# Two thirds of the r, k and v loads in rows of sixteen tokens, and a second set of decay tables

## The chip, the cores and the metric

The kernel runs on one core of a Trainium2 chip. The metric is the device time of one execution in microseconds (us), lower is better. Three executions of the kernel before took 121.07, 121.30 and 121.99 us (median 121.3).

The engines are named as in the profile: PE (TensorE, matmuls and transposes; PEld is its weight load), DVE (VectorE), ACT (ScalarE), POOL (GpSimd) and SP (which here only issues DMAs). All of them read and write the on-chip memory (SBUF); PE writes its results to a small second memory (PSUM), from which DVE and ACT copy them out ("eviction"). Sixteen DMA engines move data between HBM and SBUF.

## What is computed

The reference runs a linear-attention layer (r, k, v of 4 batches x 8 heads x 768 tokens x 48, a decay w and a bonus u per head and channel) and feeds its output, as 3072 tokens of 384 features, to a soft mixture of 8 experts with 4 slots each:

```python
for t in range(S):                                   # S = 768
    cur = einsum('bhd,bhe->bhde', u * k[t], v[t])
    y[t] = einsum('bhd,bhde->bhe', r[t], state + cur)
    state = w * state + einsum('bhd,bhe->bhde', k[t], v[t])
x = y as [3072, 384]
logits = x @ phi                                     # [3072, 32]
slot_input = softmax(logits over tokens).T @ x       # [32, 384]
slot_out[e] = relu(slot_input[e] @ w1[e]) @ w2[e]    # F = 1024, 8 experts
out = softmax(logits over slots) @ slot_out          # [3072, 384]
```

r, k and v are 14.2 MB together, w1 and w2 25.2 MB, the output 4.7 MB, all f32 in HBM.

## The kernel before

**Units.** The attention is computed in 12 units of 256 tokens, three to a batch, all heads together. A unit is two chunks of 128 tokens. For each unit n the tasks are, in the kernel's names (a task's letter, then the unit):

- `Lk Lr Lv`: three loads of 384 KB, issued by SP (line 188). A load has 32 rows of 8 tokens for each head, so it moves 256 pieces of 8 x 48 x 4 = 1536 B.
- `Sk Sr`: k and r times a table of decay powers, f32 to bf16 (line 376; on POOL, only `Sk0` on DVE). `VC`: v to bf16 (lines 402 and 404, on ACT or POOL).
- `Tk Tr Tv`: eight PE transposes each into a PSUM bank (lines 386, 412); `Ek Er Ev`: eviction to SBUF (line 328 on ACT, 326 on DVE); `PR`: the product of k and r for the bonus term (line 395, DVE).
- `N`/`NE` and `V`/`VE`: transposes back to token rows, and their eviction.
- `A`: the chunk's 128 x 128 scores, half a unit at a time (`An0`, `An1`, line 451), into one PSUM tile `Ab`; `K`: those times the causal mask, to bf16 (line 457, DVE, 24 in all).
- `U`, `SM`, `SI`, `SE`: the state's step (lines 471 to 496). `DV`: the bonus term (line 501, DVE). `Y`: the outputs (lines 513 to 524); `YE`: their eviction; `X`/`XE`: transposes for the mixture.

When a batch is through, its logits and both softmaxes follow (`L`, `ZC`, `RM`, `EX`, `NM`, `DP`, `AC` and others); `NM` ends in line 654 on DVE. After the last batch come the experts: `H` (first layer, line 803), `R`, `HT`, `HE`, and then `Q00` to `Q14` (second layer, line 848), of which `Q10` reads the second-layer weights of experts 4 and 5 (`W12`, `W13`), `Q11` those of expert 6 (`W14`), and `Q12` to `Q14` the three parts of the last one (`W15a`, `W15b`, `W15`). Then the output is computed and stored (lines 855 to 882).

**Order.** The string `ORDER` (lines 9 to 31) lists every task once; each engine runs its own tasks in that order, and `_Plan.run` (line 60) hands out the buffers in it. `Fn_m` are fillers: matmuls with no use (line 794), m/2 of 512 columns each. No engine overtakes within its own list, so a task that waits holds all that stands behind it on its engine.

**Loads and weights.** SP issues the loads in order and holds back when eight are under way. The weights (`W0` to `W15`, 768 KB each in bf16, converted by the DMA) are issued by POOL, between its other tasks. `W0` stands behind a one-element copy that waits until the v of unit 9 has landed (`GU = 9`, line 706, and line 713), so that the weights come behind the inputs; `W8` and later also wait for the weight DMA eight places earlier. Loads and weights share the buffers `raw`: 16, and the table's, which becomes free at the end.

**The start.** The table is built on chip: w arrives, ACT takes its logarithm, DVE multiplies it with exponents 0 to 8 plus the row's offset (line 256), ACT takes exponentials (lines 259 and 260). POOL waits for the last of these before `Sr0`, DVE for the first ones before `Sk0`. `CC`, `CT`, `CA`, `CU` and `CW` turn w and u into columns: `CC` (line 265) and `CA` (line 287) on DVE, `CT` on PE, `CU` (lines 290 and 291) on POOL, `CW` on ACT. `CB` (lines 313 and 314, with two ACT copies) makes constants for the mixture.

```python
        O(sp.dma_start(out=dst.rearrange("p (e x) -> p e x", e=2),
                       in_=a[b].rearrange("h (y j) d -> y h (j d)", j=J)[CC * R * i:CC * R * (i + 1)]))
...
            add(f"S{nm}{n}", "DVE" if n == i == 0 else "POOL", f_scale, deps=[f"L{nm}{n}"],
```

Of the kernel before, what the change touches and what calls it, by code (L numbers as in the profile page):

```python
# [9 lines left out]
Lk0 CB Lr0 Sk0 Tk0 Lv0 Sr0 Lk1 VC0:ACT Sk1 LU Lr1 Ek0 Sr1 F0_4 N0 Lv1 Tr0 Lk2 Lr2 Tv0 Er0 NE0:ACT CC Lv2 A01 CT  # L10
Ev0:ACT V0 VC1:ACT Lk3 PR0 CA K01 Lr3 VE0:ACT Tk1 A00 Tv1 CU Ek1 Sk2 Ev1:ACT Sr2 K00 Tr1 Lv3 Lk4 N1 CW LP Lr4 Sk3 U0
PR1 V1 Lv4 Er1 NE1:ACT VC2:ACT Tk2 A10 DV0 SM0 VE1:ACT Tv2 SI0 Lk5 Tr2 Y0 K10 Ek2 Sr3 SE0 A11 Ev2:ACT Lr5 K11 Sk4 U1
N2 Lv5 Er2:ACT PR2 Sr4 YE0 Lk6 Lr6 SM1 DV1 Lv6 VC3:ACT Lk7 Lr7 NE2:ACT VC4 Tk3 Sk5 A21 Ek3:ACT Lv7 Lk8 Tr3 Lr8
Er3:ACT Lv8 V2 Tv3 K21 SI1 Ev3:ACT Y1 Lk9 PR3 VC5 Lr9 Lv9 A31 SE1 Lk10 N3 V3 VE2:ACT YE1 Tk4 U2 K31 Lr10 CB0 VE3:ACT
Sk6 NE3 SM2 DV2 X10 Tr4 A20 Ek4:ACT XE10:ACT N4 U3 Tk5 Er4:ACT K20 A30 NE4:ACT PR4 K30 Tv4 Tv5 Ek5:ACT X00 Sr5 Y2
Lv10 Ev4:ACT VC7 A40 Tk6 Lk11 XE00:ACT CB1 N5 DV3 Ev5 SM3 Tr5 YE2 Y3 Ek6:ACT V4 NE5:ACT X20 K40 Lr11 SI3 PR5 Er5 YE3
A41 XE20 Tv7 VE4:ACT Sr6 VC6:ACT V5 SE3 Ev7:ACT VE5:ACT U4 K41 Tv6 SM4 DV4 Ev6:ACT L0 Lv11 Sk7 A50 W0 W1 RM0 N6 SI4
Tr6 ZC0 Tk7 K50 NE6:ACT EX0 A51 W2 SE4 ZT0 U5 Ek7:ACT V6 PR6 Sk8 Sr7 SU0 SM5 N7 Er6:ACT V7 K51 Y4 VE6:ACT A61
NE7:ACT VE7:ACT DV5 AL0 VC8 Sr8 VC9 Tk8 ET0 YE4 K61 Tr7 Sr10 U6 Ek8:ACT EE0:ACT A60 PR7 Er7:ACT Tv8 DP0 LC0 W3 SM6
SI6 K60 Y5 Ev8:ACT Sk9 AC0 A71 SE6 YE5 DV6 N8 NM0 Tv9 Tr8 NE8:ACT Ev9:ACT U7 LX0 Er8:ACT V8 LE0:ACT Y6 VE8:ACT YE6  # L20
Sr9 W4 K71 SM7 A80 PR8 W5 Sk11 X50 W6 XE50:ACT K80 SI7 Tk9 X30 Ek9 A70 XE30:ACT X40 N9 XE40:ACT NE9:ACT K70 Tr9 DV7
A81 SE7 L1 RM1 Sk10 VC10 Er9:ACT W7 W8 Tk11 Y7 Ek11:ACT ZC1 YE7 AL1 K81 U8 V9 PR9 VE9:ACT Tk10 N11 VC11 SM8 NE11:ACT
W9 A90 Sr11 Ek10:ACT Tr10 DV8 ZT1 K90 U9 Er10:ACT SU1 Tv10 A101 EX1 Ev10:ACT ET1 Y8 SM9 PR10 K101 W10 V10 N10 A91
W11 EE1:ACT VE10:ACT NE10:ACT W12 DV9 DP1 X60 W13 SI9 K91 Tr11 SE9 XE60:ACT A100 PR11 K100 U10 SM10 DV10 YE8 Tv11
Er11:ACT Y9 Ev11:ACT A110 K110 V11 YE9 X80 SI10 Y10 A111 VE11:ACT SE10 X70 AC1 U11 K111 SM11 XE80:ACT YE10 XE70:ACT
X90 DV11 L2 F1_3 X100 LC1 Y11 XE90:ACT XE100:ACT RM2 ZC2:DVE ZT2 AL2 L3 EX2 YE11 F2_2 X111 NM1 W14 ZC3 SU2 X110
XE111:ACT RM3 F3a_3 ET2 XE110 W15a LB4 EE2 W15b AL3 EX3 ET3 DP2 RM4 G1 EX4 G2 LC2 EE3 ET4 AC2 EE4:ACT G3 AL4 G5 DP3
AC3 DP4 GS AC4 LX1 ZT3 F4a_2 MG LE1:ACT UN F5_6 H11 H10 R11:DVE R10 H00 NM2 HT11 R00:DVE HE11 SU3 F6a_1 H01 R01:DVE
W15 LC3 LX2 HT10 F7a_1 HT00 LE2:ACT NM3 LT4 HT01 SU4 HE00 F8a_7 Q00 LX3 LC4 HE10 HE01:ACT Q01 F9_38 Q10 NM4 LX4
F10_11 Q11 F11_2 Q12 F12_2 Q13 Q14 LE4:ACT LE3  # L30
# [51 lines left out]
def kernel(  # L82
# [13 lines left out]
    B, H, S, D = r.shape  # L96
# [54 lines left out]
    pr_t = [cst.tile([128, PH, C], bf, name=f"pr{j}") for j in range(2)]  # L151
# [34 lines left out]
    def load_f(dst, a, n):  # L186
        b, i = divmod(n, U3)
        O(sp.dma_start(out=dst.rearrange("p (e x) -> p e x", e=2),
                       in_=a[b].rearrange("h (y j) d -> y h (j d)", j=J)[CC * R * i:CC * R * (i + 1)]))

# [52 lines left out]
    O(dve.tensor_copy(turn[:].rearrange("p (c q r) -> p c q r", c=CC, q=nQ), ident[:].rearrange("p (c r q) -> p c q r", c=CC, q=nQ)))  # L243
# [68 lines left out]
    def consts_b():  # L312
        O(dve.tensor_reduce(out=sel[:], in_=ident_f[:].rearrange("p (b c) -> p c b", b=B), axis=AX.X, op=ALU.add))
# [6 lines left out]
    L = _Plan(dict(raw=raw, ks=ks_t, kT=kT_t, rT=rT_t, vT=vT_t, vj=vj_t, kn=kn_t, vn=vn_t, AT=AT_t, pr=pr_t, dv=dv_t,  # L320
# [40 lines left out]
    add("CB", "DVE", lambda t: consts_b())  # L361
    xB, xTB = {}, {}
    for n in range(NU):
# [45 lines left out]
        def f_turn(t, vjb=vjb, Tb=Tb):  # L409
            src = vjb.inst[:].rearrange("p j e d -> p j (e d)")  # L410
            for jj in range(J):
                O(pe.transpose(Tb.inst[0:P2, jj * 128:(jj + 1) * 128], src[:, jj, :], turn[:]))  # L412
# [500 lines left out]
```

## Time and profile before

| | us |
|---|---|
| runs, median (lowest to highest) | 121.3 (121.07 to 121.99) |
| the profiled execution | 122.07 |
| its span in the trace | 120.3 |
| busy: PE, DVE, ACT, POOL | 102.4, 92.4, 81.8, 61.4 |
| granted PE clock, mean | 0.972 |
| DMA queue of the loads and stores (q1): 11208 packets, 18.93 MB | 43.9% of 16 engines |
| DMA queue of the weights (q0): 2592 packets, 12.58 MB written | 51.3% |

The profile is one execution of the program, recorded by the hardware. Its page lists the busy time of each engine; the span in 40 slices of 3.0 us with a digit for each engine's busy share; the DMA queues; the chain of work that ended last; and the costliest groups of instructions with what ended the idle time before them. The trace behind it can also be asked for the timeline of one engine (start, length, line, tiles, how many instructions, and idle time before it with what ended it) and for busy time, DMA share and GB/s in stretches of one's choice. The weights' GB/s count what is written as bf16; twice as much is read.

### The profile page before, as it was taken

To read this page: it belongs to the slowest core of one execution; us is meant where nothing else is said; L and a number is where in the kernel's file an instruction comes from. 1 tells how busy PE (TensorE), PEld (TensorE's weight loads), DVE (VectorE), ACT (ScalarE), POOL (GpSimd) and SP (SyncE) were. 2 spreads that over 40 slices of the span, in tenths; PEclk is the share of its full clock that TensorE was granted. 3 is DMA by queue.
4 is the path that set the end of the run, shared out by engine and by line. 5 is a ranking of instruction groups with operands and counts; after the bars stand their busy time and mean duration, and the time that the engine had idled before them with its cause. 6 is when DMAs were issued, how large, how long until landed. Compare 5 with 4: busy or idle time off the path is not lost.

```text
span 120.3 us, 4049 instructions
## 1 busy us (share of the span) xinstructions
PE 102.4 (85%) x1726; PEld 75.7 (63%) x1732; DVE 92.4 (77%) x175; ACT 81.8 (68%) x132; POOL 61.4 (51%) x75
## 2 busy tenths in 40 slices
PE   4987789999999899959999999999989999897000
PEld 1346668888888688758887788764436556673000
DVE  6947998999999999999999999988598100189000
ACT  4638699999989899869999799896235001188000
POOL 7368999999993999999996111011000000000000
PEclk9999999999999999999999999999999999999855
DMA  2999999999999999999999999999999997039994
GB/s 35 291 346 393 374 349 366 374 375 375 373 375 370 362 245 205 227 205 218 208 220 217 206 224 206 218 217 214 217 210 224 204 209 141 14 133 415 407 419 196
DMA packets 13961, 31.81 MB, mean 264 GB/s; under 512 B 1528, under 2 KB 11000, under 8 KB 13944
## 3 DMA queue, kind: packets, MB, share of 16 engines
q0 software_dynamic: 2592, 12.58, 51.3%
q1 hardware_dynamic: 11208, 18.93, 43.9%
q8 instruction: 13, 0.21, 0.7%
q10 hardware_dynamic: 144, 0.05, 0.2%
q14 instruction: 4, 0.03, 0.1%
HBM read 39.42 MB, written 4.72 MB: 367 GB/s over the span
## 4 chain that ended last, share of the span: by engine, by line
PE 61%; DVE 20%; ACT 7%; issue 3%; POOL 1%; DVEq 0%; POOLq 0%
PE T L386 7%; PE T L794 6%; PE Ab L451 5%; PE T L541 4%; PE T L412 4%; DVE AT_all L457 4%; PE T L426 3%; PE T L212 3%; PE Yb L518 3%; PE Yb L848 3%; PE Yb L513 2%; PE T L436 2%; PE Mb L848 2%; PE Yb L524 2%; DVE mix L880 2%
## 5 line engine op out<-in xcount | busy, mean ns | idle before, releaser
L376 POOL TENSOR_TENSOR mix<-raw,tabs 128x768 bf16<-128x768 f32 x23 | 41.7, 1831 | 3.6 <-DMA raw<-in_r_dram 2.4
L457 DVE TENSOR_TENSOR AT_all<-Ab,mask 128x1024 bf16<-128x1024 f32 x24 | 29.1, 1214 | 0.7 <-PE Ab L451 0.7
L328 ACT COPY mix<-T 128x1024 bf16<-128x1024 bf16 x17 | 17.0, 1030 | 0.2 <-PE T L386 0.2
L386 PE MATMUL T<-turn,mix 128*128 128x128 bf16 x192 | 15.0, 222 | 0.1
L386 PEld LDWEIGHTS <-mix 128*128 128x128 bf16 x192 | 12.0, 99 | 1.7 <-DVE mix L376 0.7
L717 POOL DMA_DIRECT2D raw<-in_moe_w_dram x10 | 5.4, 540 | 14.2 <-DMA raw<-in_moe_w_dram 14.2
L328 ACT COPY vT_all<-T 96x1024 bf16<-96x1024 bf16 x11 | 11.2, 1018 | 1.3 <-PE T L412 1.2
L501 DVE TENSOR_TENSOR dv<-vn,Mb 128x768 bf16<-128x768 bf16 x12 | 11.3, 942 | 0.0
L451 PE MATMUL Ab<-mix 64*128 64x128 bf16 x192 | 9.7, 218 | 1.8 <-DVE AT_all L457 0.7
L328 ACT CAST x<-Yb 128x768 bf16<-128x768 f32 x12 | 9.8, 814 | 0.7 <-PE Yb L524 0.6
L328 ACT COPY vn<-T 128x768 bf16<-128x768 bf16 x12 | 9.7, 810 | 0.6 <-PE T L436 0.6
L328 ACT COPY xT_all<-T 128x768 bf16<-128x768 bf16 (+1 forms) x11 | 8.6, 780 | 0.9 <-PE T L541 0.9
L856 DVE CAST so<-Mb 128x192 bf16<-128x192 f32 x1 | 0.4, 358 | 11.0 <-PE Mb L848 11.0
L328 ACT COPY LexpT<-T 128x768 bf16<-128x768 bf16 (+1 forms) x4 | 2.8, 693 | 8.7 <-PE T L697 8.7
L794 PE MATMUL T<-mix,ident 128*128 128x512 bf16 (+1 forms) x31 | 8.1, 373 | 0.3 <-issue 0.2
L451 PEld LDWEIGHTS <-mix 64*128 64x128 bf16 x192 | 5.8, 94 | 4.1 <-issue 2.2
L395 DVE TENSOR_TENSOR pr<-T,mix 128x1024 bf16<-128x1024 bf16 x12 | 8.2, 679 | 0.0
L328 ACT COPY kn<-T 128x768 bf16<-128x768 bf16 (+1 forms) x11 | 7.6, 694 | 0.4 <-PE T L426 0.3
L412 PE MATMUL T<-turn,vj 128*96 128x128 bf16 x96 | 7.4, 221 | 0.5 <-ACT vj L402 0.5
L518 PEld LDWEIGHTS <-AT_all 128*128 128x128 bf16 x192 | 6.6, 96 | 1.6
L426 PE MATMUL T<-ident,mix 128*128 128x128 bf16 x80 | 6.5, 219 | 0.4 <-DVE mix L326 0.4
L518 PE MATMUL Yb<-vn,AT_all 128*128 128x48 bf16 x192 | 6.8, 183 | 0.0
(173 smaller groups left out, 231.5 us busy)
## 6 DMA issues: line engine op xcount, KB each, us to landing
raw<-in_moe_w_dram POOLq DMA_DIRECT2D x15, 768.0 KB, 15.6
raw<-in_k_dram SPq DMA_DIRECT2D x12, 384.0 KB, 8.2
raw<-in_r_dram SPq DMA_DIRECT2D x12, 384.0 KB, 7.9
raw<-in_v_dram SPq DMA_DIRECT2D x12, 384.0 KB, 8.1
out_dram<-mix SPq DMA_DIRECT2D x3, 768.0 KB, 4.8
out_dram<-tabs SPq DMA_DIRECT2D x1, 768.0 KB, 6.7
out_dram<-AT_all SPq DMA_DIRECT2D x1, 768.0 KB
out_dram<-mix SPq DMA_DIRECT2D x1, 576.0 KB, 2.8
```

The source lines that it names most:

```text
L328: O(act.copy(dst, src))
L376: O(eng.tensor_mul(ks.inst.rearrange("p (j e s) -> p e j s", j=J, e=2)[:, :, :, 0:D], halfs(kb)[i].rearrange("p (e j d) -> p e j d", e=2, ...
L386: O(pe.transpose(Tb.inst[:, jj * 128:(jj + 1) * 128], src[:, jj, :], turn[:]))
L395: O(dve.tensor_mul(pb.inst[:].rearrange("p g (j r) -> p g j r", j=J), Tb.inst[:].rearrange("p (j g r) -> p g j r", j=J, r=R), kT.inst.rear ...
L412: O(pe.transpose(Tb.inst[0:P2, jj * 128:(jj + 1) * 128], src[:, jj, :], turn[:]))
L426: O(pe.transpose(Tb.inst[:, x * 128:(x + 1) * 128], kT.inst[:, x, :], ident[:]))
L451: O(pe.matmul(Abf.inst[:, e, x * C:(x + 1) * C], kT.inst[s, g * nQ + x, :], rT.inst[s, g * nQ + x, :]))
L457: O(dve.tensor_mul(AT.inst[:], Abf.inst[:].rearrange("p e (g t) -> p e g t", g=nQ), mask[:, None, None, :].to_broadcast([128, 2, nQ, C])))
L501: O(dve.tensor_mul(dvb.inst[:].rearrange("p g e d -> p (g e) d"), vn.inst[:].rearrange("p g e d -> p (g e) d"), Mf.inst[:, 448:448 + 2 * P ...
L518: O(pe.matmul(y[:, x // nQ, q * P2 + e * D:q * P2 + (e + 1) * D], a[x // nQ].inst[:, e, q, :], vn.inst[:, x, e, :], start=False, stop=(c = ...
L794: O(pe.matmul(o[:, 0:256 * min(n, 2)], ident[:], mix[:, 0:256 * min(n, 2)], start=True, stop=True))
L848: O(pe.matmul(SO[h][32 * x:32 * x + 32, :], hT[g][:, y, 32 * x:32 * x + 32], w2_of(g * EG + x)[:, y, h * Dm // 2:(h + 1) * Dm // 2], start ...
```

## The change

- Batches are loaded in two pieces in place of three: the first unit (256 tokens) as before in rows of 8 tokens (loads 0, 2, 4, 6), the second and third unit together in rows of 16 tokens (loads 1, 3, 5, 7): 768 KB each, 256 pieces of 3072 B. There are 24 loads in place of 36, with the same bytes.
- A long load is scaled, transposed and evicted in two halves `a` and `b`, eight of each row's sixteen tokens each. Both units of it need both halves.
- Rows of sixteen need exponents 0 to 16, and one table each for k and r (`tabl`), beside the short one (`tabs`). They are built by two more products on DVE (`AHa`, `AHb`, two instructions each) and four exponentials on ACT (`TB0a`, `TB1a`, `TB1b`, `TB0b`), inside the order.
- The buffers of transposed k, r and v are one for the short and one double one for the long load: three units' worth, where k and r had four and v two. `raw` has 14 buffers; the three tables' space is used later. `PR` has one short and one long buffer.
- `Sk` and `Sr` of the first two loads may be on DVE: `Sk1b` and `Sr1a` are. Ten of the twelve `VC` are on POOL (seven before), two on ACT.
- The exponents take four more small DVE instructions and one in a new order, the transposes' permutation two copies in place of one, and POOL makes a second one (`turnl`). A memset of a PSUM bank (line 262) moves into `CB`, which is now behind `AHb`.
- The gate of the weights waits for the v of load 6, which is unit 9's. POOL issues two weights there, then one, three, and one at a time (three, one, two, then ones and twos before).
- `ORDER` is another list. `F9_38` in front of `Q10` and `F10_11` in front of `Q11` are gone; `F9_12` stands in front of `Q11`.

```diff
-Lk0 CB Lr0 Sk0 Tk0 Lv0 Sr0 Lk1 VC0:ACT Sk1 LU Lr1 Ek0 Sr1 F0_4 N0 Lv1 Tr0 Lk2 Lr2 Tv0 Er0 NE0:ACT CC Lv2 A01 CT
-Ev0:ACT V0 VC1:ACT Lk3 PR0 CA K01 Lr3 VE0:ACT Tk1 A00 Tv1 CU Ek1 Sk2 Ev1:ACT Sr2 K00 Tr1 Lv3 Lk4 N1 CW LP Lr4 Sk3 U0
...
-W15 LC3 LX2 HT10 F7a_1 HT00 LE2:ACT NM3 LT4 HT01 SU4 HE00 F8a_7 Q00 LX3 LC4 HE10 HE01:ACT Q01 F9_38 Q10 NM4 LX4
-F10_11 Q11 F11_2 Q12 F12_2 Q13 Q14 LE4:ACT LE3
+AHa TB0a Lk0 Sk0 Tk0 Lr0 TB1a AHb Sr0 Lv0 Ek0:ACT CB VC0 F0_3 Tr0 N0 Lk1 Er0 TB1b LU TB0b Tv0 Lr1 Ev0:ACT PR0 Sk1a
+CC Sk1b:DVE A01 CT NE0:ACT CA Lv1 CU K01 V0 Lk2 Lr2 Sr1b Tk1b Sr1a:DVE VE0:ACT A00 VC1a Tk1a CW Lv2 U0 K00 Tr1a SM0
+Ek1b:ACT VC1b Ek1a:ACT Tr1b Er1a PR1a Lk3 Lr3 SI0 LP Er1b:ACT Sk2 Tv1a Ev1a:ACT Lv3 A10 Lk4 Tv1b DV0 N1 Lr4 K10 Lv4
...
+H00 R11:DVE R10 R00:DVE LC4 HT11 F5a_1 H01 HE11 HT10 HE10:ACT F6a_3 LX3 R01:DVE HT00 LE3 HE00 F7a_1 HT01 NM4 F8_1
+LX4 Q00 HE01 Q01 Q10 F9_12 Q11 F10_2 Q12 F11_2 Q13 Q14 LE4:ACT LE2:ACT
...
-    R = 16
+    R = 8
     J = C // R
+    JH = J // 2
...
-    NRAW, NKS, NX = 16, 6, 2
-    raw = [big.tile([128, 2 * RW], f32, name=f"raw{j}")[:] for j in range(NRAW)]
-    tabs = big.tile([128, 2, 2, J, D], f32, name="tabs")
+    RH = RW // 2
+    NRAW, NKS, NX = 14, 6, 2
+    raw = [big.tile([128, RW], f32, name=f"raw{j}")[:] for j in range(NRAW)]
+
+    tabs = big.tile([128, 2, 2, JH, D], f32, name="tabs")
+    tabl = [big.tile([128, 2, J, D], f32, name=f"tabl{j}") for j in range(2)]
...
+    turned = dict(ks=cells(mix, 6, 1), kl=cells(mix, 7, 2), rs=cells(mix, 9, 1), rl=cells(mix, 10, 2),
+                  vs=cells(vT_all[0:P2], 0, 1), vl=cells(vT_all[0:P2], 1, 2))
...
-    def load_f(dst, a, n):
-        b, i = divmod(n, U3)
-        O(sp.dma_start(out=dst.rearrange("p (e x) -> p e x", e=2),
-                       in_=a[b].rearrange("h (y j) d -> y h (j d)", j=J)[CC * R * i:CC * R * (i + 1)]))
+    def load_f(dst, a, m):
+        b, lg = divmod(m, 2)
+        jn = J if lg else JH
+        O(sp.dma_start(out=dst[:, 0:2 * jn * D].rearrange("p (e x) -> p e x", e=2),
+                       in_=a[b].rearrange("h (y j) d -> y h (j d)", j=jn)[lg * CC * R:lg * CC * R + 32]))
...
+    def argv_part(dst, ex):
+        n = ex.shape[1]
+        for e in range(2):
+            O(dve.tensor_mul(dst[:, e], lnw.rearrange("p (e d) -> p e d", e=2)[:, e, None, :].to_broadcast([128, n, D]),
+                             ex[:, :, None].to_broadcast([128, n, D])))
...
+    for h, av_, x in (("a", argl, slice(0, JH + 1)), ("b", argm, slice(JH, J + 1))):
+        add(f"AH{h}", "DVE", (lambda av_, x: lambda t: argv_part(av_, e17l[:, x]))(av_, x))
+        for i in range(2):
+
+            add(f"TB{i}{h}", "ACT", (lambda i, h, av_: lambda t: O(act.activation(
+                out=tabl[i][:, :, JH:J] if h == "b" else tabl[i][:, :, 0:JH],
+                in_=av_[:, :, 1 - i:JH + 1 - i], func=AF.Exp, scale=(-1.0, 1.0)[i])))(i, h, av_),
+                deps=["AHa", "AHb"][:1 + (h == "b")], bufs=[tabB[1 + i]])
...
+                    add(sd, "DVE" if nm == "k" and m == 0 else "POOL DVE" if m < 2 else "POOL", f_src,
+                        deps=[f"L{nm}{m}"] + [f"TB{i}{hx}"] * lg, bufs=[kr[nm, m][0], src, tabB[(1 + i) * lg]])
...
-    GU = 9
+    GU = "v", NLD - 2
```

More of the change, by code (lines that the diff above doesn't have):

```diff
@@ L409, in f_turn @@
[L409 to L412, printed above, removed]
-        add(f"Tv{n}", "PE", f_turn, deps=[f"VC{n}"], bufs=[vjb, Tb])
-        def f_ev(t, Tb=Tb, vT=vT):
-            ev(t, vT.inst.rearrange("p g (j r) -> p g j r", j=J),
-               Tb.inst[0:P2, :].rearrange("p (j g r) -> p g j r", j=J, r=R))
-        add(f"Ev{n}", "DVE ACT", f_ev, deps=[f"Tv{n}"], bufs=[Tb, vT])
+        m = 2 * bt + (ui > 0)
```

220 lines of the change are left out of this document (120 added, 100 removed).

## The prediction

> **What bounds the kernel now.** I read the page's 40 slices first, then stretches near the end, then the queues of SP and POOL, then PE and DVE in order of time. The slices (3.0 us each) show DMA engines without a pause from the second slice to slice 33:
>
> ```profile
> DMA  2999999999999999999999999999999997039994
> GB/s 35 291 346 393 374 349 366 374 375 375 373 375 370 362 245 205 227 205 218 208 220 217 206 224 206 218 217 214 217 210 224 204 209 141 14 133 415 407 419 196
> ```
>
> Loads run at 375 GB/s, weights at 215 (written; 430 read), stores at 414. Issues by line give the weights' last three parts with KB and the time to landing, POOL's timeline their issue:
>
> ```profile
> raw<-in_moe_w_dram POOLq DMA_DIRECT2D x1, 384.0 KB, 28.3
> raw<-in_moe_w_dram POOLq DMA_DIRECT2D x1, 288.0 KB, 25.6
> raw<-in_moe_w_dram POOLq DMA_DIRECT2D x1, 96.0 KB, 22.9
> ```
>
> ```profile
> 74.20 0.53 POOL L717 DMA_DIRECT2D raw<-in_moe_w_dram  x1 [2.90 <-DMA raw<-in_moe_w_dram]
> 78.33 0.53 POOL L717 DMA_DIRECT2D raw<-in_moe_w_dram  x1 [3.60 <-DMA raw<-in_moe_w_dram]
> 81.56 0.53 POOL L717 DMA_DIRECT2D raw<-in_moe_w_dram  x1 [2.71 <-DMA raw<-in_moe_w_dram]
> ```
>
> They land at 102.5, 103.9 and 104.5. PE's timeline shows who meets them (start, length, line):
>
> ```profile
> 94.19 4.28 PE L794 MATMUL T<-mix,ident 128*128 128x512 bf16 x18
> ...
> 104.57 0.25 PE L848 MATMUL Yb<-raw,AT_all 128*32 128x192 bf16 x1
> ```
>
> PE is through with `Q01` at 94.2, burns 4.3 us of `F9`, and `Q14` starts 0.1 us after its weights. So the stream of DMAs sets the end, and the computation arrives some 5 us early, all of it filler: `Q14` ends at 104.75. The computation itself has little air. In stretches of busy time (PE, PEld, DVE, ACT, POOL, then granted clock, DMA share, GB/s):
>
> ```profile
> 12.00:80.00 68.00, 64.48 (x1344) 53.51 (x1341) 66.55 (x97) 62.97 (x91) 53.21 (x54) 1.00 1.05 284
> 109.00:118.00 9.00, 1.53 (x7) 0.73 (x5) 2.55 (x6) 1.75 (x4) 0.00 (x0) 0.75 1.02 414
> ```
>
> DVE idles 1.45 us in 68. Whatever delays DVE at the start reaches `Q01`.
>
> **The loads.** SP's timeline shows the pace, since each issue waits for a landing eight places earlier:
>
> ```profile
> 21.55 0.60 SPq L188 DMA_DIRECT2D raw<-in_r_dram  x1
> 22.61 0.60 SPq L188 DMA_DIRECT2D raw<-in_v_dram  x1
> 23.66 0.60 SPq L188 DMA_DIRECT2D raw<-in_k_dram  x1
> ```
>
> A load of 256 pieces takes 1.055 us: 16 pieces on each of 16 engines, 65.9 ns for 1536 B. The stores, rows of 6144 B at 414 GB/s (25.9 on an engine), take 237 ns a row. The line through both has 9 ns fixed and gives 123 ns for 3072 B; through the weights (12288 B read at 430 GB/s, 457 ns) it gives 122. A long load then takes 1.96 us, two short ones 2.11. Twelve times 0.15 is 1.8 us. Bounds: 0, if the rate hangs on bytes alone, and 2.5 if 9.44 MB run at 414 in place of 373. I take 1.8, between two rows that agree.
>
> The weights follow the inputs without a gap, so they land 1.8 earlier: the three parts at 100.7, 102.1, 102.7, and `Q14` could end at 102.9. That needs the stream fed. By POOL's rows (1.81 us an `S`, 0.82 a `VC`, 0.6 an issue) its list reaches the gate near 39.0 (now 38.6). Six loads' worth follow it, so inputs last until 38.6 + 6 x 1.055 - 1.8 = 43.1. `W0` to `W2` hold 3 x 3.66 us (768 KB at 215 GB/s), until 54; `W3` is issued near 49.7, and data flow some 2 us after an issue. Margin 2 us; cover gone, each us late costs one. SP's list is not held by buffers: its last loads reuse space that POOL reads by 24, and issue near 30. Twelve loads fewer save only SP time, which hides behind the transfers.
>
> **The start.** Five small DVE instructions (0.10 to 0.29 each by the present ones) and a second permutation copy put the first product of the tables at 4.5, now 3.69. `AHa` (1.1, by line 256) stands where `CB` and the memset (1.0) stood; so `Sk0` starts at 6.9, now 5.85, and `Sr0` at 7.0, now 6.41, behind the last exponential. `Ek0` goes to ACT behind `TB0a` and `TB1a` (0.8 each, by line 260) and ends at 9.9, now 8.6; it is not late. DVE has `AHb` 1.1, `CB` 1.0, `Er0`, `PR0`, then `CC`. `Sk1b` needs `TB0b`, which on ACT is behind `Ek0`, two copies and `TB1b`: 11.95. So `Sk1b` 12.0 to 12.9, `CA`, `K01` to 14.2, `Sr1a` to 15.1, `K00` to 16.3; now it ends at 14.9. That is 1.4 late if nobody is in the way. k and r of the long load land by 12.5 (v of unit 0 at 8.5 by ACT's wait, plus 1.96 each), just in time.
>
> But these rows say somebody is. Twice an operation of DVE that reads only SBUF took much longer while POOL scaled:
>
> ```profile
> 5.32 0.19 DVE L265 COPY wu<-LexpT 4x96 f32<-4x96 f32 x1
> 10.35 1.07 DVE L265 COPY wu<-LexpT 4x96 f32<-4x96 f32 x1
> ...
> 51.43 2.17 DVE L654 TENSOR_TENSOR Lc<-Ls,sm 128x192 bf16<-128x192 f32 x1
> 79.20 0.36 DVE L654 TENSOR_TENSOR Lc<-Ls,sm 128x192 bf16<-128x192 f32 x1
> ```
>
> POOL's scalings then ran from 9.54 (two of 1.8) and from 49.78 (3.59 for two), and both DVE operations ended just after one of them. `AHb`, `Sk1b` and `Sr1a` are of that kind. The Trainium skill, "SBUF — State Buffer", section "Who interferes with whom", says so: a VectorE instruction with two SBUF inputs and a GpSimd one that reads SBUF exclude each other for a whole instruction. The trace agrees (0.36 to 2.17).
>
> With that: `Sr0` waits for `Sk0` (7.8) and ends at 9.5, and `AHb` waits for it, 1.7 us, holding `CB`, `Er0` and all DVE behind, and through `CB`'s result and `AHb` itself the exponentials that `Sk1b` waits for: `Sk1b` ends 14.3. `CA` releases `CU` and then `Sr1b` on POOL, which holds `Sr1a` for another 1.2: `K00` ends at 18.9, 4.0 late; 4.8 if `VC0` gets between the two halves of `AHb`. I take 4.0: in the first row DVE came in at the next boundary between two scalings.
>
> **Behind it.** From `K00` to the last batch DVE has the same work in both lists, 83 tasks, 62.5 and 62.6 us by the rows' starts. PE, ACT and POOL are delayed less, so DVE's 1.45 us of idling can go (bounds 0 and 1.45); I take it all, since each of those waits was for PE. Fewer transposed buffers cost nothing: at a change of batch, `Er3b` waits for `Y2`, but DVE has 6.4 us of other tasks between. `Y11` stands 1.0 later in DVE's work, and from `UN` to `Q01` DVE has about 1.0 less (`NM2`, `SU3`, `NM3` stand before `UN`): nothing together.
>
> So `Q01` ends at 94.2 + 4.0 - 1.45 = 96.75. From there PE has `Q10` 1.44, `F9_12` 6 x 0.238 = 1.43, `Q11` 1.43, fillers 0.64, `Q12` 0.76, `Q13` and `Q14` 0.71: 6.4 us, to 103.15. The weights allow 102.9. The tail behind `Q14` (15.5 us of span) is the same. Sum: 103.15 - 104.75 = -1.6 us.
>
> **Rivals.**
> 1. DVE stays late in part, `Q01` at 97.3 to 98.3 (4.8 late, 0.7 to 1.45 recovered, or 4.0 and none): end 103.7 to 104.7, -1.05 to 0. For it: the four long rows; against: the lists leave PE and ACT ahead. About 120.8.
> 2. DVE stays late in full: 4.8, nothing recovered, and `Y11`'s 1.0 not returned: `Q01` at 100.0, end 106.4, +1.65, 122.95. It decides where `Q01` passes 98.35, since 6.4 later is 104.75. For it: the same rows, and POOL and DVE meet in SBUF at least twice.
> 3. Loads gain nothing: the weights' bound stays, 121.3. For it: bytes moved are the same. Against: 414 GB/s with longer rows. The Trainium skill, "DMA: Bandwidth & Descriptors", section "Where 436 GB/s comes from", has HBM bind a core's transfers at about 358 GB/s, under which longer rows would gain nothing. By that rule the sum is 0; the trace's 375, 414 and 430 speak against it.
> 4. POOL is over 2 us later than I think, and the weights run dry near 54; 5 us late gives 3 - 1.8, +1.2 or 122.5.
>
> **How the numbers follow.** The profiled execution took 122.07, its span 120.3; the sum applies to it (120.5) and to the median alike: 121.3 - 1.6 = 119.7. Chances: forecast (-1.2 to -1.9) 0.46, rival 1 0.21, rival 2 0.15, rival 3 0.10, rival 4 0.08. The range takes the bound 2.5 of the loads at its low end, 118.8, and reaches to 122.2 through rivals 1 and 3 and half of 2 and 4. About 1% (1.2 us) can be told from no change. Faster: the forecast and a little of rival 1, 0.48. Same: the rest of 1, 3, the edges of 2 and 4, 0.35. Slower: 0.17.
>
> **What would show it.** Two long loads' issues 1.96 us apart; the last weights landing near 102.7; `K00` (the second operation of the causal mask) starting near 17.7, or 15.1 without the port; `AHb`, `Sr1a` or POOL's scalings beside them longer than 1.1, 0.94 and 1.81; DVE without idling behind; PE waiting for weights after `Q10`, if at all. The forecast is wrong if the long loads take 2.1, if `Q01` ends after 98, or if the DMA share falls below 1 between 40 and 100.

## The result, and the profile after

The changed kernel took 127.92 us (median of 4, 127.31 to 129.03) against 121.64 (median of 4) for the kernel before on the same chip: 1.052 times as long, 95% interval 1.042 to 1.062. The prediction said 119.7, with a range to 122.2. The profiled execution took 127.31, its span 125.5. Every ratio here and in the table below leaves out executions more than 1.5% above the fastest of their kernel, as medians and traces do not: e2_expo and e4_short keep two of four, and three kernels that keep one have no ratio.

The 40 slices of the page (3.1 us each):

```profile
PEclk9999599999999999999558999999999999999755
DMA  2999999999998999999999999999999940029994
GB/s 38 325 345 413 384 397 369 378 397 390 381 399 331 161 219 213 211 196 221 217 210 210 217 215 217 215 217 213 213 217 212 202 83 5 0 86 415 407 421 174
```

Two things differ from before. The loads run near 390 GB/s where they ran near 374, and ahead of the stores the DMA engines now pause for two slices (5 and 0 GB/s), before for one (14): the stream no longer sets the end. And PE's granted clock, 1.0 without a break up to the tail before, is 0.5 in a slice near 13 us and in two from 60 on.

The last issue of POOL, and how long it took to land, by the issues of the page:

```profile
81.62 0.53 POOL L764 DMA_DIRECT2D raw<-in_moe_w_dram  x1 [3.09 <-DMA raw<-in_moe_w_dram]
```

```profile
raw<-in_moe_w_dram POOLq DMA_DIRECT2D x1, 96.0 KB, 21.8
```

That is 103.4, before 81.56 + 22.9 = 104.5. PE meets the weights late now. Its timeline around the end of `Q01`, and DVE's first copy behind `Q14`:

```profile
104.62 0.25 PE L895 MATMUL Mb<-raw,AT_all 128*32 128x192 bf16 x2
105.04 1.24 PE L841 MATMUL T<-mix,ident 128*128 128x512 bf16 x5 [0.16 <-issue]
```

```profile
109.91 0.36 DVE L903 CAST so<-Mb 128x192 bf16<-128x192 f32 x1 [7.79 <-PE Mb L895]
```

and the same copy in the kernel before:

```profile
104.93 0.36 DVE L856 CAST so<-Mb 128x192 bf16<-128x192 f32 x1 [10.97 <-PE Mb L848]
```

`Q01` ends at 104.9 in place of 94.2, 10.7 late, behind all weights. The fillers (1.24 at 105.04) now burn time with nothing left to wait for. The copy of `so` starts at 109.9, before at 104.9: that is the 5 us.

Where do the 10.7 come from? DVE's timeline of the start:

```profile
2.73 1.49 DVE L245 CAST pf<-pl 128x17 f32<-128x17 int32 x1
...
5.97 1.11 DVE L278 TENSOR_TENSOR AT_all<-LexpT,e 128x432 f32<-128x432 f32 x2
...
16.49 2.28 DVE L420 TENSOR_TENSOR mix<-raw,tabl 128x768 bf16<-128x768 f32 x1
18.69 1.21 DVE L504 TENSOR_TENSOR AT_all<-Ab,mask 128x1024 bf16<-128x1024 f32 x1
```

and `K00` in the kernel before:

```profile
13.74 1.20 DVE L457 TENSOR_TENSOR AT_all<-Ab,mask 128x1024 bf16<-128x1024 f32 x1
```

The conversion of 17 numbers took 1.49 us; the same one for the first table, a microsecond earlier, 0.17. POOL copied `turnl` and wrote zeros beside it until 4.19. The first product starts at 5.97, `Sr1a` takes 2.28 (0.94 alone), and `K00`, the second operation of the causal mask, starts at 18.69, before at 13.74: 4.95 late.

In the middle, DVE's timeline around `NM0`, the division of the first batch's softmax (line 701, 654 before), and POOL's and PE's beside it:

```profile
56.73 3.59 DVE L701 TENSOR_TENSOR Lc<-Ls,sm 128x192 bf16<-128x192 f32 x1
60.24 0.54 DVE L543 TENSOR_TENSOR S<-Mb,wT 128x384 bf16<-128x384 f32 x1
...
62.11 0.56 DVE L532 TENSOR_TENSOR Z<-Mb,wT 128x384 bf16<-128x384 f32 x1 [0.19 <-PE Mb L525]
63.13 0.56 DVE L732 COPY acc<-T 128x385 f32<-128x385 f32 x1 [0.47 <-PE T L725]
...
66.10 0.42 DVE L677 TENSOR_REDUCE rm<-T 128x1 f32<-128x256 f32 x1 [0.61 <-ACT zc L353]
```

```profile
55.91 3.58 POOL L420 TENSOR_TENSOR mix<-raw,tabl 128x768 bf16<-128x768 f32 x2
59.43 0.59 POOL L762 DMA_DIRECT2D raw<-in_moe_w_dram  x1
```

```profile
60.84 0.48 PE L518 MATMUL Mb<-S,ident 128*128 128x192 bf16 x2 [3.10 <-DVE S L543]
```

An instruction that takes 0.36 alone took 3.59, to the end of two scalings and an issue of POOL. `SE6`, queued behind it, releases PE, which had waited 3.1 us; and in the stretch that follows (columns as before)

```profile
59.90:66.70 6.80, 5.86 (x78) 3.96 (x78) 5.12 (x10) 2.56 (x4) 6.56 (x8) 0.50 1.03 212
```

PE has half its clock, and DVE in turn waits for PE and ACT, 1.9 us in five waits up to 72.1. The account at `Q01`, in DVE's time: 4.95 at `K00`; from the end of `K00` to the start of `RM3` (a maximum taken for a softmax, at 88.54) 68.64 us in place of 65.26, of which 1.70 is busy time (the division 1.42) and 1.68 idle; from there to the end of `Q01` 16.33 in place of 14.04. Together 10.6 of the 10.7.

### The profile page after: what moved, and what is told of

Its sections match the earlier page's. It is cut to its first block, busy times and chain, and to the rows that moved or that the text cites. A ratio compares the mean times of both kernels' runs of the same rounds, so it can differ in the third digit from the quotient of the medians.

```text
span 125.5 us, 3992 instructions
## 1 busy us (share of the span) xinstructions
PE 100.6 (80%) x1706; PEld 76.1 (61%) x1709; DVE 99.3 (79%) x182; ACT 84.8 (68%) x137; POOL 62.6 (50%) x77
## 4 chain that ended last, share of the span: by engine, by line
PE 46%; DVE 35%; ACT 6%; POOL 3%; issue 3%; DVEq 0%
PE T L429 10%; DVE AT_all L504 7%; PE Ab L499 4%; DVE Lc L701 3%; DVE mix L927 3%; PE T L474 3%; POOL mix L420 3%; PE T L484 3%; PE Yb L565 3%; PE Yb L895 2%; PE Yb L560 2%; DVE pr L445 2%; PE Mb L525 2%; PE Mb L895 2%; PE T L841 2%
## 5 line engine op out<-in xcount | busy, mean ns | idle before, releaser
L420 POOL TENSOR_TENSOR mix<-raw,tabl 128x768 bf16<-128x768 f32 x14 | 25.4, 1823 | 0.2
L353 ACT COPY mix<-T 128x1024 bf16<-128x1024 bf16 x18 | 18.1, 1019 | 1.0 <-PE T L429 0.9
L420 POOL TENSOR_TENSOR mix<-raw,tabs 128x768 bf16<-128x768 f32 x7 | 14.3, 2042 | 4.3 <-ACT tabs L285 4.3
L429 PE MATMUL T<-turnl,mix 128*128 128x128 bf16 x128 | 9.1, 219 | 0.7 <-DVE mix L420 0.7
L764 POOL DMA_DIRECT2D raw<-in_moe_w_dram x8 | 4.4, 550 | 10.1 <-DMA raw<-in_moe_w_dram 10.1
L411 POOL CAST vj<-raw 128x768 bf16<-128x768 f32 x10 | 8.8, 897 | 0.0
L353 ACT COPY xT_all<-T 128x768 bf16<-128x768 bf16 (+1 forms) x10 | 7.4, 782 | 0.2 <-PE T L588 0.2
L429 PE MATMUL T<-turn,mix 128*128 128x128 bf16 x64 | 5.4, 233 | 1.9 <-POOL mix L420 1.8
L429 PEld LDWEIGHTS <-vj 128*96 128x96 bf16 x96 | 6.5, 129 | 0.6
L532 DVE TENSOR_TENSOR Z<-Mb,wT 128x384 bf16<-128x384 f32 x12 | 6.6, 548 | 0.3 <-PE Mb L525 0.3
```

Of the source, the lines that this page charges most:

```text
L353: O(act.copy(dst, src))
L411: O(act.copy(o, i_) if t.eng == "ACT" else pool.tensor_copy(o, i_))
L420: O(eng.tensor_mul(src.inst.rearrange("p (j e s) -> p e j s", j=JH, e=2)[:, :, :, 0:D], rv(), tab))
L429: O(pe.transpose(Tb.inst[0:P, jj * 128:(jj + 1) * 128], sv[:, jj, :], (turn, turnl)[lg][:]))
L532: O(dve.tensor_mul(Smid.inst[:], Mf.inst[:, 0:SW].rearrange("p (q d) -> p q d", q=nQ)[:, :, None, :].to_broadcast([128, nQ, 2, D]), wT[:, ...
```

## The experiments

All start from the changed kernel unless said. The table gives, of each profiled execution, the start of `K00`, the length of `NM0`'s division, the landing of the last weights and the start of the `so` copy; then the median of all executions, and the ratio to the kernel before.

| | time profiled | `K00` | division | weights | `so` | median | ratio (95%) |
|---|---|---|---|---|---|---|---|
| before | 122.07 | 13.74 | 2.17 | 104.5 | 104.93 | 121.6 | |
| changed | 127.31 | 18.69 | 3.59 | 103.4 | 109.91 | 127.92 | 1.052 (1.042 to 1.062) |
| e1_nm0 | 123.39 | 18.75 | 1.12 | 103.3 | 105.99 | 123.91 | 1.018 (1.012 to 1.024) |
| e2_expo | 130.08 | 18.00 | 5.42 | 104.2 | 112.69 | 129.22 | 1.049 (1.043 to 1.055) |
| e3_fill | 124.88 | 18.60 | 3.58 | 103.3 | 107.49 | 131.07 | |
| e4_short | 129.94 | 18.39 | 5.42 | 104.4 | 112.54 | 129.29 | 1.050 (1.043 to 1.057) |
| e5_front | 123.63 | 15.77 | 0.36 | 103.3 | 106.25 | 123.31 | 1.011 (1.005 to 1.018) |
| e6_cut | 121.86 | 18.58 | 1.11 | 103.0 | 104.42 | 121.83 | 1.002 (1.000 to 1.005) |
| e7_all | 122.31 | 15.89 | 0.36 | 102.6 | 104.91 | 122.32 | 1.003 (0.999 to 1.006) |
| e8_bnm0 | 125.38 | 13.97 | 0.36 | 104.0 | 108.15 | 123.32 | 1.011 (1.006 to 1.016) |
| e9_end | 122.91 | 18.65 | 0.72 | 103.1 | 105.53 | 121.70 | 1.000 (0.997 to 1.003) |
| e10_end_short | 121.77 | 18.36 | 0.99 | 104.2 | 104.62 | 121.71 | 1.003 (0.999 to 1.006) |
| e11_ms | 120.52 | 17.34 | 0.59 | 102.7 | 103.14 | 120.98 | 0.997 (0.994 to 1.000) |
| e12_both | 120.71 | 17.34 | 0.36 | 102.8 | 103.30 | 120.91 | 0.994 (0.991 to 0.997) |
| e13_fill2 | 132.18 | 18.37 | 7.37 | 103.9 | 114.79 | 132.53 | |
| e14_nm0_back | 127.64 | 17.64 | 5.50 | 102.4 | 110.25 | 127.69 | |
| e15_sr1a | 120.95 | 16.81 | 0.36 | 103.2 | 103.55 | 121.79 | 1.002 (0.996 to 1.007) |
| e16_both_short | 122.09 | 17.34 | 1.45 | 104.4 | 104.76 | 121.73 | 1.001 (0.996 to 1.005) |

**The division's place** (e1_nm0):

```
-... XE7:ACT NM0 SE6 A71 ...
+... SE6 A71 ...
...
-... Y7 K80 A81 ...
+... Y7 K80 NM0 A81 ...
```

> Only the division NM0 is moved on DVE, from in front of SE6 to behind K80, where POOL has no scaling left. Theory A (DVE's lateness sets the end, and the division held behind POOL's two scalings costs more than its own 3.2 us because PE, ACT and then DVE itself run dry behind it): the division takes 0.36 us, DVE's waits between 60 and 72 us (2.1 us now) go too, PE's clock stays at 1.0 there, and the end comes 3.2 to 5.3 us earlier: 122.0 to 124.1. Theory B (the lateness of the start alone decides, and the middle has slack behind it): the division is short, but the time stays within 0.6 of 127.3. Theory C (POOL's scalings hold whichever DVE operation of two SBUF inputs comes next): DV7 or another gets the 3 us, time 126 to 127.5.

```profile
63.40 1.12 DVE L701 TENSOR_TENSOR Lc<-Ls,sm 128x192 bf16<-128x192 f32 x1
```

The division took 1.12 (not 0.36), DVE's long waits behind it went, the clock stayed at 1.00 there, and `so` came 3.9 us earlier, more than the 2.5 that the division itself got shorter. Theory A holds. The same edit taken out again from a kernel mended elsewhere (e14_nm0_back, compare e11_ms):

> e11_ms (median 120.98, profiled 120.52) with the division NM0 back in its old place in front of SE6, all else kept. Theory A (the place of the division alone costs its block and what runs dry behind it, in any kernel of this family): the division takes 3.4 to 5.4, PE's clock falls behind it, and the time is 3 to 5.5 us more, 124 to 126.5. Theory B (an earlier start lets it through between two scalings): the division takes under 1.9 and the time stays under 122.5.

Its four executions took 124.65 to 131.43; the traced one has the division at 5.50 and `so` 7.1 us later than e11_ms. Their median is 6.7 us above e11_ms's and the fastest 3.7: one place in a list of DVE is worth some 4 us and more.

**PE's clock** (e3_fill and, the same kernel again, e13_fill2):

```
-... X50 U7 XE40:ACT XE50:ACT XE30:ACT DP0 ...
+... X50 XE40:ACT XE50:ACT XE30:ACT F20_26 U7 DP0 ...
```

> 13 filler matmuls of 512 columns (about 2.9 us of PE) are put where PE idles 3.1 us behind the blocked NM0; nothing else. Theory A (the granted clock of 0.5 between 60 and 67 us follows from that idling, and costs DVE part of its 2.1 us of waits): the clock stays at 1.0 there, PE's transposes take 0.6 and not 1.1 us, and the time falls by 0.5 to 1.5. Theory B (the clock drops, but DVE's waits come from ACT and from the list): clock 1.0, time within 0.4 of 127.3. Theory C: the clock still drops, so idling is not what it follows.

> The kernel of e3_fill once more, since its four times (124.88, 131.66, 131.99, 130.48) fell apart and only the shortest left a trace. Theory A (the fillers keep PE's clock up and that is worth about 2.4 us; the long executions had the division held by three scalings, 5.4 us, or another stretch at half clock): a trace of an execution near 130 shows the division at 5.4 or a stretch of 0.5 elsewhere. Theory B (the fillers themselves delay PE): such a trace shows PE still busy with fillers when SE6 is through.

The trace of e3_fill has the same division (3.58), and for the same stretch as above (59.9 to 66.7)

```profile
59.90:66.70 6.80, 6.80 (x139) 4.95 (x137) 6.66 (x12) 4.44 (x7) 6.67 (x9) 1.00 1.05 216
```

the full clock, PE without a pause and DVE with hardly any, and `so` 2.4 us earlier. Theory A holds for this trace: against the changed kernel's, with `K00` (18.60) and the division as late, 2.4 of the 5.0 us by which `so` was late came by way of the clock. That is one pair of executions. But the seven other executions of this kernel took 126 to 133, and the trace of one at 132.18 shows why that one did:

```profile
57.81 7.37 DVE L701 TENSOR_TENSOR Lc<-Ls,sm 128x192 bf16<-128x192 f32 x1
```

```profile
56.65 3.59 POOL L420 TENSOR_TENSOR mix<-raw,tabl 128x768 bf16<-128x768 f32 x2
60.17 0.59 POOL L762 DMA_DIRECT2D raw<-in_moe_w_dram  x1
60.78 1.81 POOL L420 TENSOR_TENSOR mix<-raw,tabl 128x768 bf16<-128x768 f32 x1
62.53 0.59 POOL L764 DMA_DIRECT2D raw<-in_moe_w_dram  x1
63.15 1.81 POOL L420 TENSOR_TENSOR mix<-raw,tabl 128x768 bf16<-128x768 f32 x1
```

```profile
59.02 2.97 PE L841 MATMUL T<-mix,ident 128*128 128x512 bf16 x13 [0.21 <-ACT xT_all L353]
65.70 0.48 PE L518 MATMUL Mb<-S,ident 128*128 128x192 bf16 x2 [3.71 <-DVE S L543]
```

DVE got through only when POOL's last scaling was done, at 65. The fillers bridged three microseconds, PE idled 3.7 more, and the clock fell after all. The wait is not until the next boundary between two scalings: the division got in behind the second one at 3.6, behind the third at 5.4 to 5.5 (e2, e4, e14), behind the fourth at 7.4. What decides the number is open. The Trainium skill, "SBUF — State Buffer", section "Who interferes with whom", has whichever of the two starts first hold the ports for its whole instruction; by these traces the one that waits can lose several instructions in a row, and they decide. The Trainium skill, "TensorE: Matmul & The Clock Gate", section "What's actually happening", has PE's clock halved after an idle window of some 3.4 us. The traces agree that it falls when PE idles (3.1 us idle and 6.8 us at 0.50 in the changed kernel, 1.00 with the gap filled), but not on the length: in the changed kernel it fell 2.2 us after PE's last matmul, and in e12_both it fell near 16 us, to 0.50 for 6.8, with no gap above 1.3 us ahead of it. So a filled gap is no guarantee of the clock.

**The start.** First the exponents alone (e2_expo):

```
     expos(e17, nQ * (2 * R - 1), float(JH // nQ))
-    expos(e17l, nQ * (R - 1), float(J // nQ))
...
     for t in ks_t:
         O(dve.memset(t.rearrange("p (x s) -> p x s", s=64)[:, :, D:64], 0.0))
+    expos(e17l, nQ * (R - 1), float(J // nQ))
```

> Only the second set of exponents is computed later on DVE, behind the six memsets of the ks buffers, so that its conversion from int32 no longer stands 1.49 us behind POOL's memsets. First product of the tables at 4.7 in place of 5.97. Theory A (lateness at the start passes one to one to the end): K00 starts 1.2 us earlier, 17.4, and the time falls by 1.0 to 1.3, to 126.2. Theory B (POOL's scaling Sr0 and the waits for Tr0 set the start): K00 gains less than 0.4 and the time stays at 127.3. Theory C (the meeting of NM0 with POOL's scalings depends on when DVE gets there): the division's 3.59 us change by more than 0.5 in either direction and the time with it.

The first product came 0.9 earlier (5.06), not 1.3: the copies of `turn`, now in the place of the conversion, took 1.82 in place of 0.33. `K00` gained 0.7. The ratio does not differ from the changed kernel's, and the median of all four is longer (129.22). In the traced execution PE ran at 0.50 from 9.6 to 19.6 and the division took 5.42, so theory C is what this trace shows, and the question of theory A stayed open.

e5_front, on top of e1_nm0, reorders the start (`NM0` now behind `K81`), puts the second exponents where e2_expo has them, and adds matmuls with no use at the start (`keep_warm(14)` for `keep_warm(9)`, and `F0_10`):

```
-... TB1a AHb Sr0 Lv0 Ek0:ACT CB VC0 F0_3 Tr0 ... CC Sk1b:DVE A01 CT NE0:ACT CA Lv1 CU K01 V0 Lk2 Lr2 Sr1b Tk1b Sr1a:DVE ... U0 K00 Tr1a SM0
+... TB1a Sr0 Lv0 Ek0:ACT CB AHb VC0 F0_10 Tr0 ... CC A01 CT NE0:ACT K01 Lv1 V0 Sk1b:DVE A00 CA Sr1b CU Lk2 Lr2 Tk1b ... K00 Sr1a:DVE U0 Tr1a SM0
```

> On top of e1_nm0 (NM0 now behind K81): the second exponents behind the memsets, AHb behind CB so that Sr0 is not held, K01 ahead of Sk1b, Sr1a behind K00, CU behind Sr1b, and 12 more filler matmuls at the start. Theory A (lateness of DVE at the start passes one to one to the end while the weights leave room): the second mask product and Sr1a are through by 17.0 to 17.6 in place of 20.0, so the time falls by 2.4 to 3.0 from e1's 123.4 profiled (123.9 median), to 120.4 to 121.5; there the weights (landing near 103) begin to bind, so no less than 120.4. Theory B (some other stage, PE or ACT, sets the pace behind the start): the start is earlier, Q01 is not, time 122.5 to 124.

`K00` came 3.0 earlier and the end did not (106.25 against 105.99). Part of the start was only moved (`AHb` took 2.42 there, behind POOL), PE had a clock of 0.54 from 17 to 24, and DVE then waited 0.66, 0.42 and 1.24 us for PE. By this run alone, an earlier start would be worth nothing. e11_ms, which changes no order, says otherwise. On top of e6_cut (below), it takes the zeros from POOL:

```
+    O(act.copy(Lc_t[0][:], warm[:, None, 0:128].to_broadcast([128, NS, 128])))
     O(act.activation(out=lnw, in_=w_f, func=AF.Ln))
+    O(act.copy(acc[:], warm[:, 0:Dm + 1]))
...
-    for t in (Lc_t[0], selp, nm_t[1], acc):
+    for t in (selp, nm_t[1]):
         O(pool.memset(t[:], 0.0))
```

> e6_cut with POOL's memsets of Lc and acc (0.73 and 0.42 us, at 2.9 to 4.2) replaced by two copies of a zeroed tile on ACT, which idles there. Theory A (DVE's conversion at 2.73 is held by these memsets, and the lateness of the start passes on): the conversion takes 0.3 to 0.6 in place of 1.49, the first product starts near 4.8 in place of 5.9, the second mask product 1.0 to 1.2 earlier (17.5), and the end as much, down to the weights' floor: 120.6 to 120.9. Theory B (POOL, busy without a pause from 12 to 64, and PE set the pace behind the start, as e5_front suggested): the start is earlier, the time within 0.4 of e6's 121.8.

DVE's timeline in e6_cut, and then in e11_ms:

```profile
2.71 1.49 DVE L246 TENSOR_SCALAR pf<-pf 128x17 f32<-128x17 f32 x1
...
5.75 1.11 DVE L278 TENSOR_TENSOR AT_all<-LexpT,e 128x432 f32<-128x432 f32 x2
```

```profile
2.47 0.20 DVE L245 CAST pf<-pl 128x17 f32<-128x17 int32 x1
2.71 0.46 DVE L246 TENSOR_SCALAR pf<-pf 128x17 f32<-128x17 f32 x1
...
4.72 1.10 DVE L278 TENSOR_TENSOR AT_all<-LexpT,e 128x432 f32<-128x432 f32 x2
```

In e6_cut the conversion already took 0.20, and the multiplication of the same 17 numbers behind it was held, 1.49; here it takes 0.46. The first product starts 1.0 earlier than in e6_cut, `K00` 1.24 earlier, `so` 1.28 earlier, and the median falls from 121.83 to 120.98 (the intervals of the two ratios only touch, at 1.000). Theory A: with the order kept, the start's lateness passed on one to one; in e5_front, which changes the order, it did not. `K00` is still 3.6 later than before there; it no longer shows, since the weights land earlier and the fillers are fewer.

The last of the prediction's port waits, `Sr1a` behind POOL's `Sr1b`, on top of e12_both (below):

```
-... NE0:ACT CA Lv1 CU K01 V0 Lk2 Lr2 Sr1b Tk1b Sr1a:DVE VE0:ACT ...
+... NE0:ACT CA Sr1a:DVE Lv1 CU K01 V0 Lk2 Lr2 Sr1b Tk1b VE0:ACT ...
```

> e12_both with Sr1a in front of K01 on DVE, before POOL's Sr1b has begun. Theory A (Sr1a is held 1.3 us by Sr1b): it takes 0.94 in place of 2.26, the second mask product starts 1.0 to 1.3 earlier (16.1 to 16.3), and the time falls by 0.2 to 0.8 from e12's 120.9 to where the weights stop it (last landing near 102.5, 120.2 to 120.7). Theory B (POOL's Sr1b is held in its place, and its list passes it on): K00 earlier, the time within 0.3 of 120.9 or above.

`Sr1a` took 0.94 and `K00` started 0.5 earlier, but DVE then waited 0.49, 0.31, 0.20 and 0.65 us for PE and POOL, and the median was 121.79. The time is theory B's, its mechanism is not: POOL's `Sr1b` was not held (1.81), only the first of `CU`'s two operations was (0.79 in place of 0.20). The wait was real, but removing it there moved it.

**The end of the list.** e6_cut is e1_nm0 with fewer fillers:

```
-LX4 Q00 HE01 Q01 Q10 F9_12 Q11 F10_2 Q12 F11_2 Q13 Q14 LE4:ACT LE2:ACT
+LX4 Q00 HE01 Q01 Q10 F9_1 Q11 F10_1 Q12 F11_1 Q13 Q14 LE4:ACT LE2:ACT
```

> e1_nm0 with the fillers behind Q01 cut from 16 quarter columns' units to 3 (F9 12 to 1, F10 and F11 2 to 1 each, 13 x 0.108 = 1.4 us). Theory A (in e1 the weights have landed at 103.0 and nothing waits for them, so the fillers lie on the path): the copies of so start 1.4 earlier, 104.6, time 122.0 to 122.5. Theory B (the last weights still bind): PE idles in front of Q13 or Q14 where the fillers were, time 123 to 124.

`so` came 1.57 earlier: theory A. With two edits of the list, neither of which touches loads or tables, the changed kernel is as fast as the kernel before (1.002). e9_end goes on from it:

```
-... HE10:ACT F6a_3 LX3 R01:DVE HT00 LE3 HE00 F7a_1 HT01 NM4 F8_1 LX4 Q00 HE01 Q01 Q10 ...
+... HE10:ACT F6a_3 R01:DVE HT00 HE00 HT01 HE01:ACT F7a_1 Q00 LX3 LE3 Q01 NM4 Q10 LX4 ...
```

> e6_cut with the end of the list in another order: LX3, LE3, NM4 and LX4 behind Q00 in place of in front of it, HE01 on ACT. Theory A (between UN and Q01 the changed list loses 1.3 us to its order, not to DVE's work): Q00 starts at 96.4 to 96.8 in place of 97.97, and the copies of so at 103.1 to 103.4 in place of 104.42, where the last weights (landing at 102.7) stop it; time 120.5 to 120.9, 0.6 to 1.0% less than before. Theory B (the work itself takes that long): Q00 stays near 97.9 and the time at 121.8.

Its median did not move, and the traced execution (122.91) had PE's clock at 0.83 on the mean from 88 to 98, in which `Q00` came at 98.50, later than in e6_cut. In e10_end_short, with the same list, `UN` to `Q00` took 6.29 in place of e6_cut's 7.44 (`Q00` at 96.60). The order is worth 1.15 us in the trace where the clock held. Together with e11_ms:

> e9_end and e11_ms together. Theory A: the weights' floor, 120.4 to 120.9. Theory B (PE's clock or a new meeting of DVE and POOL takes some back): 121.2 to 122.

0.6% less than before, interval 0.3 to 1.0%: it beats both kernels, but not e11_ms by more than can be told. e7_all, which had the front of e5_front instead, came out like e6_cut, as its theory B has it:

> e5_front and e6_cut together. Theory A: DVE's path would allow 3.9 to 4.4 less than e1, but the weights land near 103.0 and Q14 with the tail of 15.6 us of span (and 1.8 outside it) puts the floor at 120.4 to 120.9; the time is 120.4 to 121.2, 0.5 to 1.3 less than before on the same chip (121.9), which is what the longer packets are worth once DVE is out of the way. Theory B (the clock at the start or a new meeting of DVE and POOL takes it back): 122 to 124.

**The packets alone.** In e4_short, e10_end_short and e16_both_short a long load is two DMAs of half rows:

```
-        O(sp.dma_start(out=dst[:, 0:2 * jn * D].rearrange("p (e x) -> p e x", e=2),
-                       in_=a[b].rearrange("h (y j) d -> y h (j d)", j=jn)[lg * CC * R:lg * CC * R + 32]))
+        for h in range(1 + lg):
+            x = slice(h * JH * D, (h + 1) * JH * D)
+            O(sp.dma_start(out=dst[:, 0:2 * jn * D].rearrange("p (e x) -> p e x", e=2)[:, :, x],
+                           in_=a[b].rearrange("h (y j) d -> y h (j d)", j=jn)[lg * CC * R:lg * CC * R + 32, :, x]))
```

> Each long load is split into two DMAs with packets of 1536 B; tables, units and lists stay those of the changed kernel. This takes away the longer packets alone. Theory A (the long packets do save 0.15 us a long load, but the end is DVE's): two DMAs of 1.05 to 1.06 us take the place of one of 1.96, the last weights land 1 to 2 us later (104.5 to 105.5), and the time stays within 0.6 of 127.3. Theory B (the weights still matter): the time rises by 1 or more. Theory C (the rate hangs on bytes alone): the two together take 1.96 as well and nothing changes anywhere.

> e9_end with each long load split into two DMAs of 1536 B packets: the longer packets alone are taken away, in a kernel whose end is near that of the weights. Theory A (the weights set e9's end): the last weights land 0.7 to 1.3 us later than in e9, as they did in e4_short against the changed kernel, and the time is 0.7 to 1.2 more than e9's: 121.3 to 122.0. Theory B (DVE and PE still set the end): within 0.4 of e9.

> e12_both with each long load split into two DMAs of 1536 B packets. Theory A (in e12 the weights are within 0.5 us of setting the end): the last weights land at 103.5 to 103.9 in place of 102.57, PE waits for them, and the time is 0.5 to 1.1 more than e12's 120.9: 121.4 to 122.0, which is what the longer packets are worth. Theory B: within 0.3 of e12.

Between 20 and 40 us, the changed kernel and then e4_short (last number GB/s):

```profile
20.00:40.00 20.00, 19.42 (x401) 16.85 (x401) 19.60 (x28) 18.70 (x24) 20.00 (x21) 1.00 1.04 387
```

```profile
20.00:40.00 20.00, 19.55 (x403) 16.97 (x403) 19.60 (x28) 18.50 (x24) 20.00 (x20) 1.00 1.07 369
```

The long rows carry 387 GB/s, the short ones 369 (385 to 388 in every trace with long rows, 368 or 369 in the three with short ones), and the last weights land 1.0 later (104.4; in the traces with long rows they range from 102.4 to 104.2). In e4_short the time does not tell: its ratio and the changed kernel's overlap, its median is 1.4 longer, and the traced execution has the division at 5.42. In e10_end_short it does not follow: 121.71 against e9_end's 121.70, theory B, although PE waited 0.18 and 0.36 us for weights there. In e16_both_short it does: 121.73 against e12_both's 120.91, and PE waited for weights near the end:

```profile
103.90 0.24 PE L899 MATMUL Yb<-raw,AT_all 128*32 128x192 bf16 x1 [0.38 <-DMA raw<-in_moe_w_dram]
```

So by the medians the longer rows' own gain is some 0.8 us in e12_both's kernel (the two intervals overlap by a hair), and none shows in e9_end's. The trace of e16_both_short has only this 0.38 of waiting; its `Q00` came 1.0 later than e12_both's, with PE's clock at 0.84 from 88 to 98, so how much of the 0.8 the rows are worth by themselves is not shown.

**The kernel before with its own division moved** (e8_bnm0; `NM0`, `LX0` and `LE0` in front of `SU1`):

> The kernel before, with its own division NM0 (2.17 us, 1.8 of them behind POOL), the transposes LX0 and the copy LE0 behind it moved to where POOL has no scaling left (in front of SU1). Theory A (there the stream of weights sets the end and DVE has some 4 us to spare): DVE reaches the last mask product 1.5 to 2 us earlier, the fillers in front of the last weights absorb it, the last weights land at 104.4 as they did, and the time stays within 0.5 of 121.9. Theory B (DVE sets the end there too): the time falls by 1.5 to 1.8.

Neither theory: it became 1.1% slower than the kernel before. The division took 0.36, but in the traced execution DVE then waited for PE (0.76, 0.44, 0.77 and 1.88 us between 53 and 72), the clock fell in slices near 14 and 69, and `Q00` came 3.2 later than before. The fillers behind `Q01` are run whether or not the weights have landed, so that lateness went to the end. Only one execution, above the median, left a trace; what the others lost is open.

## Why the prediction was wrong, by its steps

- **What bounds the kernel before: right as read, not as used.** The computation was 5 us early, but in fillers of a fixed number: whoever is late at `Q01` gains only what the list drops of them. The prediction did count the changed list's own fillers.
- **"I take 1.8" for the loads: right in mechanism, 1.1 in size.** 387 GB/s against 374, and the last weights 1.1 earlier. Part of the rest is the rate (14.2 MB at 387 in place of 374 save 1.3, an estimate), part the feeding: between 40 and 50 us the DMA share was 0.96, before 1.06. Not at `W3`, where the prediction saw its margin of 2 us, but at the first weights: they were issued at 39.8, and from 40 to 41 the share was 0.37, so the inputs did not last until 43.1. In e11_ms, 1.2 earlier at the start, the share is 1.04 and the weights land at 102.7, as predicted; in e15_sr1a, also at 1.04, they land at 103.2.
- **The start, "4.0 late": 4.95.** The wait of `Sr1a` was right (2.28). The other meeting went the other way round: `AHb` was not held (1.11), POOL's `Sr0` was (3.35), and DVE idled 1.65 for the transposes behind it. The mis-sized term was "five small DVE instructions (0.10 to 0.29 each by the present ones)": one took 1.49, beside POOL's zeros, and one 0.45, and the first product started at 5.97 in place of 4.5.
- **"DVE's 1.45 us of idling can go ... I take it all": this step failed most.** DVE idled 3.13, not 0, and was busy 1.7 longer; from `K00` to `RM3` that is 4.8 of the 8.1 by which `Q01` missed 96.75. The prediction quoted the row of the division at 2.17, and priced the same conflict for the new products, but kept the division itself at its old price, though the change moved it against POOL's list. e1_nm0 and e14_nm0_back show its price; the one trace of e3_fill puts 2.4 us of it on the clock, which the prediction did not have at all.
- **"From `UN` to `Q01` DVE has about 1.0 less: nothing together": failed by 2.3.** `UN`, which makes the experts' input, came 0.9 later behind `RM3`, about as the prediction has it, but from `UN` to `Q01` it took 10.24 in place of 8.86, 1.4 more and not 1.0 less. That stage is not DVE's work alone but a chain of PE, ACT and DVE in turn. The order of `LX3`, `LE3`, `NM4` and `LX4` cost 1.15 of that (e10_end_short against e6_cut, to `Q00`).
- **"6.4 to 103.15" from `Q01`: 5.0**, the only term that came out better.
- **The rivals.** Rival 1's lower bound for `Q01` should read 97.55 (94.2 + 4.8 - 1.45), not 97.3; nothing hangs on it. Rival 2 had the right kind of loss and the right point from which it decides (98.35), but 100.0 for `Q01` where it was 104.9. Rival 3 fell by the rate (387 against 369, packets alone). Rival 4's weights ran a little thin, without setting the end.

## What to carry to other kernels

A change that moves one engine's list moves every pair of instructions that share a resource: go through the long rows of the trace before, and price each of them again at its new neighbours, not only the instructions that are new. Price a wait through its queue: a division 2.5 us shorter was worth 3.9 at the end (e1_nm0), since PE idles behind it and then runs slower. And cut fillers when the transfer that they cover gets shorter.

## What the runs showed of the hardware

- A product of two SBUF inputs on DVE, 0.36 alone, waited 3.2, 5.1 and 7.0 us beside back-to-back scalings of POOL, past two to four of them and the DMA issues between. 3.58 and 7.37 are two executions of one kernel.
- POOL's writing of zeros held a conversion of 17 numbers for 1.3 us (1.49 against 0.20), or the multiplication behind it (1.49 against 0.46), or a pair of bf16 copies for 1.5 (1.82 against 0.33), but not DVE's memsets: six took 0.87 in the kernel before, beside POOL's, and 0.87 in e11_ms, without.
- Executions of one kernel differ: the changed kernel spread over 1.7 us, e14_nm0_back over 6.8, e6_cut, where the division is not held for long, over 1.1. The two traces of one kernel (124.88 and 132.18) differ in the division and in where PE's clock halves. The mean clock alone does not order the times: e12_both has 120.15 at 0.936 and 121.43 at 0.969.
